# Second pair's K^T K apart from K^T Q, larger first loads, a shorter norm root, a clamp on another engine, and a redrawn order

## The chip, the core and the metric

The kernel runs on one core of a Trainium2 chip. The core has a matrix engine (TensorE, PE in the profile, with PEld for its weight loads), VectorE (DVE), ScalarE (ACT), GpSimd (POOL) and SyncE (SP), which here only issues DMA transfers. POOL issues DMA transfers too. Each engine works through its own instructions in order and waits on semaphores for the others. The metric is the time of one execution on the device in microseconds (us).

## The reference

A layer of linear attention with the delta rule, and behind it a gated causal convolution:

```python
B, H, S, D = 4, 8, 768, 48
k_n = k / (norm(k, axis=-1) + 1e-6)
for t in range(S):
    y[:, :, t] = einsum('bhd,bhde->bhe', q[:, :, t], state)
    v_old = einsum('bhde,bhd->bhe', state, k_n[:, :, t])
    state += beta[t] * outer(k_n[t], v[t] - v_old)
x = y.transpose(0, 2, 1, 3).reshape(4, 768, 384)
gate = sigmoid(sum_k conv_w[k] * shift(x, 4 - k))        # 5 taps, causal, per channel
out = (gate * (x @ w_val)) @ w_out
```

The convolution's and the output layers' weights arrive as float64, as pairs of 32-bit words, and are put together as fp32 on the chip.

## The kernel before, in words

**Tiling.** The 768 tokens are cut into 12 chunks of 64, two chunks are a pair (six pairs, `NG`). The 32 sequences (4 batches of 8 heads) fill the partitions and the free axis. Within a chunk the recurrence is solved as a triangular system; between chunks the state is carried.

**The stages of a pair `g`** (names as in the code):

- `grams`: K^T K and K^T Q of both chunks on PE. For pairs under `NAL` (only pair 0) they are separate products (`kp`, `qp`); for the others one joint product (`kq`, two per chunk, each with K as the stationary side and K and Q side by side as the moving side). ACT copies K^T K into `GL` (`kpevac`, `kqevac`), DVE multiplies K^T Q by a mask into `AQ` (`att0`, `att`). For pair 0 DVE realigns parts of `GL` (`kpfix`); for the others SP does it by DMA (`realign`).
- `prep`, nearly all on DVE: a transposition of `GL` into `TLP` (`trans_in`), then 18 small steps on 128x32 (`coef`), which take the norm's inverse root by three Newton steps of three operations each and make the coefficients, then `cscale`, `row`, `mergez8`, `merget8`, which invert the small triangular blocks, and two transpositions (`trans_out`) into `XA` and `WB`. ACT (pair 0) or POOL (other pairs) copies them on as `XAB` (`xblocks`) and `W` (`wblocks`); SP writes the diagonal blocks of `GL` into `G` (`gblocks`).
- `tri`, per chunk: the products `m16`, `m32`, `lev1`, `lev2` on PE with ACT copies between them; they end in `XX`.
- `chain`, per chunk: `e` (K times state, PE), `eadd` (DVE), `u` (PE, `XX` times V), `s` (the next state, PE), `y` (PE), ACT copies between them, and six small DMA transfers by SP (kind `Lx`) that put patches of `YSB` into x (`X`).
- `moe`, per pair: five taps of the convolution (one as an ACT copy, four as DVE operations on three blocks each), sigmoid on ACT, `val` on PE, `gate` on DVE, `outp` on PE, `oevac` on ACT, output by SP.

**The weights** (`plan_weights`, seven of them: the convolution's, 128x15, then three blocks each of `w_val` and `w_out`, 128x384): SP loads the words, then `f64_bits` runs step 0 on ACT and steps 1 to 4 on DVE (step 1 is a clamp by max and min), `f64_low` runs on ACT, and `f64_join` on POOL. Two buffers are used in turn, taken from `X`, `OS` and `GT`.

**Loads.** K and Q of a chunk come in halves of 48x512 (96 KB each, `load_k`, `load_q`), four DMA transfers each. The first four chunks (`NSP`) are loaded by SP, the later ones by POOL.

**What sets the order.** All operations are collected in a plan and numbered. The list `ORDER` gives the order in which they are emitted, for all engines at once, and `BANKS` gives the bank of PSUM of each product. An entry of -1 in `ORDER` emits one small matmul on constants (`keep_warm`); the list before has none. In the trace each fp32 matmul counts as two.

Of the kernel before, what the change touches and what calls it, by code (L numbers as in the profile page):

```python
# [19 lines left out]
NP = 16  # L20
NU = 32
HB = 8
NAL = 1
# [88 lines left out]
]  # L112
BANKS = (
    "2301451005500150542334121020310011111441044230325245334254224345034420352123140133255103053104224032150552400423"
    "013100412454031514230541552034323314055305340203512432524224043210012143115341040405012052022053124"
)


# [931 lines left out]
```

## Time and profile before

| | |
|---|---|
| runs | 312.48, 313.34, 319.33 us; median 313.34 |
| profiled execution | 315.52 us, its span 313.8 us |
| granted PE clock, mean | 0.88 |
| busy: PE, PEld | 258.8 us (82%), 194.6 us (62%) |
| busy: DVE, ACT, POOL | 215.5 us (69%), 168.5 us (54%), 115.2 us (37%) |
| HBM read, written | 21.35 MB, 4.72 MB |

The shares are means over the span; the stages differ. The timeline views list an instruction's start and length, and in square brackets the time that its engine had been idle before it and what ended that idle time. The windows view gives the busy time of each engine in a stretch, beside the PE clock that was granted in it (1.00 is the full clock, 0.50 the half).

### The profile page before, as it was taken

To read this page: it belongs to the slowest core of one execution; us is meant where nothing else is said; L and a number is where in the kernel's file an instruction comes from. 1 tells how busy PE (TensorE), PEld (TensorE's weight loads), DVE (VectorE), ACT (ScalarE), POOL (GpSimd) and SP (SyncE) were. 2 spreads that over 40 slices of the span, in tenths; PEclk is the share of its full clock that TensorE was granted. 3 is DMA by queue.
4 is the path that set the end of the run, shared out by engine and by line. 5 is a ranking of instruction groups with operands and counts; after the bars stand their busy time and mean duration, and the time that the engine had idled before them with its cause. 6 is when DMAs were issued, how large, how long until landed. Compare 5 with 4: busy or idle time off the path is not lost.

```text
span 313.8 us, 14806 instructions
## 1 busy us (share of the span) xinstructions
PE 258.8 (82%) x6422; PEld 194.6 (62%) x6422; DVE 215.5 (69%) x504; ACT 168.5 (54%) x404; POOL 115.2 (37%) x230
## 2 busy tenths in 40 slices
PE   7410996567679897999997899898999799999994
PEld 4310885457555576965767875577657598656772
DVE  5799539996479897289983099993999701664480
ACT  1900666556559544484555477354666446774531
POOL 8844207244516393502669102767012451000000
PEclk9855577567999999599999799999999857999999
DMA  5697727363558464534586535873226272304033
GB/s 152 177 221 184 207 48 194 100 157 67 134 138 167 96 173 115 148 73 115 134 227 150 133 59 122 251 168 75 56 81 157 79 173 55 92 17 119 15 101 75
DMA packets 55937, 39.29 MB, mean 125 GB/s; under 512 B 38592, under 2 KB 46912, under 8 KB 55872
## 3 DMA queue, kind: packets, MB, share of 16 engines
q1 hardware_dynamic: 50752, 25.76, 33.8%
q0 software_dynamic: 5120, 12.59, 15.4%
q8 instruction: 50, 0.82, 1.2%
q14 instruction: 15, 0.12, 0.1%
HBM read 21.35 MB, written 4.72 MB: 83 GB/s over the span
## 4 chain that ended last, share of the span: by engine, by line
PE 48%; DVE 4%; ACT 3%; DMA 3%; issue 2%; SPq 2%; POOL 2%; ACTq 0%; POOLq 0%; DVEq 0%
PE PB L242 23%; PE PB L688 13%; PE PB L697 10%; SPq L229 2%; DMA X<-YSB 2%; DMA Y<-US 2%; PE SPS L242 1%; ACT Y L224 1%; DVE PR L490 1%; POOL XAB L226 1%; ACT OS L224 1%; DVE PR L502 1%; DVE VT L623 1%; ACT X L224 0%; DVE TT__81 L483 0%
## 5 line engine op out<-in xcount | busy, mean ns | idle before, releaser
L679 DVE SCALAR_TENSOR_TENSOR GT<-X,CW,GT 128x512 f32<-128x512 f32 (+1 forms) x84 | 54.0, 678 | 15.5 <-ACT GT L224 14.4
L242 PE MATMUL PB<-KQ 48*64 48x128 f32 (+1 forms) x896 | 35.7, 310 | 18.9 <-DMA KQ<-in_kf_dram 14.2
L697 PE MATMUL PB<-WO,GT 128*128 128x384 f32 x144 | 50.7, 497 | 0.7 <-DVE GT L692 0.7
L688 PE MATMUL PB<-X,WV 128*128 128x512 f32 (+1 forms) x126 | 49.7, 541 | 1.7 <-DMA X<-YSB 1.7
L224 ACT ACTIVATE XX<-PB 32x512 f32<-32x512 f32 (+1 forms) x72 | 36.9, 518 | 22.3 <-PE PB L242 21.5
L242 PEld LDWEIGHTS PB<-KQ 48*64 48x64 f32 x896 | 30.4, 168 | 21.9 <-issue 15.5
L405 DVE TENSOR_TENSOR AQ<-PB,MASK 128x256 f32<-128x256 f32 (+1 forms) x44 | 18.5, 442 | 31.7 <-ACT GL L224 15.7
L697 PEld LDWEIGHTS PB<-WO,GT 128*128 128x128 f32 x144 | 26.1, 189 | 16.8 <-DVE GT L692 1.3
L688 PEld LDWEIGHTS PB<-X,WV 128*128 128x128 f32 x126 | 22.9, 190 | 19.9 <-issue 15.5
L571 POOL TENSOR_TENSOR VT<-VT,NRM 128x384 f32<-128x384 f32 x24 | 20.6, 859 | 26.9 <-DMA VT<-in_vt_dram 14.0
L224 ACT ACTIVATE Y<-SPS 64x384 f32<-64x384 f32 (+1 forms) x44 | 20.4, 482 | 16.9 <-PE SPS L242 16.6
L242 PE MATMUL PB<-KQ,Y 112*48 112x64 f32 (+2 forms) x768 | 28.1, 236 | 0.1
L242 PEld LDWEIGHTS PB<-KQ,Y 112*48 112x48 f32 (+2 forms) x768 | 25.7, 136 | 2.5 <-issue 1.3
L623 DVE TENSOR_TENSOR VT<-PB,VT 128x384 f32<-128x384 f32 x22 | 11.5, 547 | 22.2 <-PE PB L242 22.2
L242 PE MATMUL PB<-YS,W 128*64 128x64 f32 x384 | 18.0, 258 | 5.5 <-issue 2.1
L232 POOL DMA_DIRECT2D VT<-in_vt_dram x16 | 9.0, 566 | 34.0 <-PE PB L242 22.7
L242 PEld LDWEIGHTS PB<-YS,W 128*64 128x64 f32 x384 | 16.1, 169 | 7.6 <-issue 3.4
L242 PE MATMUL PB<-XAB,G 128*64 128x32 f32 x384 | 16.8, 249 | 4.2 <-POOL XAB L226 3.7
L224 ACT ACTIVATE X<-PB 112x256 f32<-112x256 f32 (+1 forms) x24 | 11.6, 488 | 16.1 <-PE PB L242 13.7
L232 POOL DMA_DIRECT2D KQ<-in_kf_dram x32 | 16.8, 527 | 8.8 <-PE PB L242 8.6
L224 ACT ACTIVATE GL<-PB 128x256 f32<-128x256 f32 (+1 forms) x44 | 16.1, 396 | 6.6 <-PE PB L242 5.2
L242 PEld LDWEIGHTS PB<-XAB,G 128*64 128x64 f32 x384 | 15.9, 171 | 5.5 <-POOL XAB L226 4.6
(106 smaller groups left out, 462.6 us busy)
## 6 DMA issues: line engine op xcount, KB each, us to landing
KQ<-AQ SPq DMA_DIRECT2D x48, 128.0 KB, 3.2
out_dram<-OS SPq DMA_DIRECT2D x20, 192.0 KB, 2.1
KQ<-in_kf_dram POOLq DMA_DIRECT2D x32, 96.0 KB, 4.2
KQ<-in_qr_dram POOLq DMA_DIRECT2D x32, 96.0 KB, 3.7
VT<-in_vt_dram POOLq DMA_DIRECT2D x16, 192.0 KB, 4.3
KT<-in_kt_dram POOLq DMA_DIRECT2D x16, 192.0 KB, 4.1
Y<-US SPq DMA_DIRECT2D x24, 96.0 KB, 2.8
KQ<-in_kf_dram SPq DMA_DIRECT2D x16, 96.0 KB, 2.6
```

The source lines that it names most:

```text
L224: A.activation(out=out, in_=in_, func=AF.Copy, **kw)
L226: eng.tensor_copy(out=out, in_=in_)
L229: SP.dma_start(out=dst, in_=src)
L232: G.dma_start(out=dst, in_=src)
L242: PE.matmul(p, lhsT, rhs, start=start, stop=stop, tile_position=(row, col), skip_group_check=True)
L405: V.tensor_tensor(out=AQ[ch % NAQ][:, HB * h + u:HB * h + u + n], in0=p, in1=MASK[h].unsqueeze(1).to_broadcast([128, n, C]), op=ALU.mult)
L490: V.tensor_tensor(out=pr[:, b], op=ALU.mult, in0=l16[:, b, 8:16, 4 * kb:8].unsqueeze(1).to_broadcast([128, 4, 8, n]), in1=t16[:, b, 4 * kb ...
L571: G.tensor_tensor(out=v, in0=v, in1=n.unsqueeze(2).to_broadcast([128, HB, D]), op=ALU.mult)
L623: V.tensor_tensor(out=v, in0=bank["e", ch, h][:, 0:HB * D], in1=v, op=ALU.add)
L679: V.scalar_tensor_tensor(out=g, in0=XB[p % NX][:, m, :, lo + k:lo + k + n], scalar=CW[:, m, k:k + 1], in1=g, op0=ALU.mult, op1=ALU.add)
L688: PE.matmul(d[:, 0:B * n], WV[:, k, 128 * m:128 * m + 128], XB[p % NX][:, k, :, lo + 4:lo + 4 + n], start=k == 0, stop=k == NKT - 1)
L697: PE.matmul(bank["out", p, lo, i][:, 0:DM], g[:, i] if n == 2 * C else g[:, 2 * i:2 * i + 2].rearrange("p b t -> p (b t)"), WO[:, k, :], s ...
```

## The change

1. `NAL` is 2: pair 1 has separate K^T K and K^T Q products as well (`kp`, `qp`), 64 matmuls more than before (128 of 64x64 in place of 64 of 64x128). Its realignment stays with SP's DMA transfers, but they now wait for the two chunks' K^T K only.
2. The first four chunks' K and Q are loaded whole (192 KB, 48x1024): 16 SP transfers fewer.
3. The norm root takes one step of third order and one Newton step in place of three Newton steps: 16 operations on DVE in place of 18 for each pair. The coefficients are scaled so that the factors stand in the later steps.
4. Step 1 of `f64_bits`, the clamp, runs on POOL instead of DVE, for all seven weights.
5. `ORDER` and `BANKS` are drawn anew. The list has 1530 entries in place of 1562, and four of them are `keep_warm`, which stand before the `u` of chunk 5, behind the `s` of chunk 5, behind the `m32` of chunk 6 and before the `lev2` of chunk 8.

```diff
--- before.py
+++ after.py
@@ -20,7 +20,7 @@
 NP = 16
 NU = 32
 HB = 8
-NAL = 1
+NAL = 2
 NSP = 4
 QB = 4
 DM = H * D
@@ -36,83 +36,81 @@
 STORE = [LATE + EARLY, EARLY + LATE]
 
 ORDER = [
-    227, 25, 29, 0, 23, 24, 21, 22, 26, 11, 16, 40, 41, 37, 38, 39, 36, 35, 34, 356, 43, 42, 164, 47, 45, 44, 264, 49,
...
 ]
 BANKS = (
...
 )
 
 
@@ -297,7 +295,7 @@
         if step == 0:
             A.activation(out=a, in_=hi.bitcast(F32), func=AF.Abs, scale=2.0 ** 16)
         if step == 1:
-            V.tensor_scalar(out=a, in0=a, scalar1=F64_LO, scalar2=F64_HI, op0=ALU.max, op1=ALU.min)
+            G.tensor_scalar(out=a, in0=a, scalar1=F64_LO, scalar2=F64_HI, op0=ALU.max, op1=ALU.min)
         if step == 2:
             V.tensor_scalar(out=ai, in0=ai, scalar1=3, scalar2=None, op0=ALU.logical_shift_left)
         if step == 3:
@@ -323,7 +321,7 @@
         hold = SCRATCH[slot]
         add("SP", load, (SCR[slot][:, 0:2 * n].bitcast(U32), src.bitcast(U32)), r=first if i else [], w=[raw, *hold], kind="Lw")
         for step in range(5):
-            add("DVE" if step else "ACT", f64_bits, (n, slot, step), r=[raw, *hold], w=[parts], 
+            add(("ACT", "POOL", "DVE", "DVE", "DVE")[step], f64_bits, (n, slot, step), r=[raw, *hold], w=[parts], 
                 kind=f"f64_{step}" + "c" * (not i))
         add("ACT", f64_low, (w, n, slot), r=[raw, *hold], w=[to], kind="f64_low" + "c" * (not i))
         for step in range(2):
@@ -427,24 +425,30 @@
                             op0=ALU.logical_shift_right, op1=ALU.bitwise_xor)
         if step == 2:
             V.tensor_scalar(out=ROOT, in0=ROOT, scalar1=ROOT_SEED, scalar2=None, op0=ALU.mult)
-        if step in (3, 6, 9):
+        if step in (3, 7):
             V.tensor_tensor(out=QUOT, in0=ROOT, in1=ROOT, op=ALU.mult)
-        if step in (4, 7, 10):
-            V.scalar_tensor_tensor(out=QUOT, in0=QUOT, scalar=-0.5, in1=SQ, op0=ALU.mult, op1=ALU.mult)
-        if step in (5, 8, 11):
+        if step == 4:
+            V.tensor_tensor(out=QUOT, in0=QUOT, in1=SQ, op=ALU.mult)
+        if step == 5:
+            V.scalar_tensor_tensor(out=QUOT, in0=QUOT, scalar=-10.0 / 3.0, in1=QUOT, op0=ALU.add, op1=ALU.mult)
+        if step == 6:
+            V.scalar_tensor_tensor(out=ROOT, in0=QUOT, scalar=5.0, in1=ROOT, op0=ALU.add, op1=ALU.mult)
+        if step == 8:
+            V.scalar_tensor_tensor(out=QUOT, in0=QUOT, scalar=-0.5 * 0.375 * 0.375, in1=SQ, op0=ALU.mult, op1=ALU.mult)
+        if step == 9:
             V.scalar_tensor_tensor(out=ROOT, in0=QUOT, scalar=1.5, in1=ROOT, op0=ALU.add, op1=ALU.mult)
+        if step == 10:
+            V.scalar_tensor_tensor(out=ROOT, in0=SQ, scalar=0.375, in1=ROOT, op0=ALU.mult, op1=ALU.mult)
+        if step == 11:
+            V.tensor_scalar(out=ROOT, in0=ROOT, scalar1=1e-6, scalar2=None, op0=ALU.add)
         if step == 12:
-            V.tensor_tensor(out=ROOT, in0=SQ, in1=ROOT, op=ALU.mult)
+            V.tensor_tensor(out=QUOT, in0=ROOT, in1=ROOT, op=ALU.mult)
         if step == 13:
-            V.tensor_scalar(out=ROOT, in0=ROOT, scalar1=1e-6, scalar2=None, op0=ALU.add)
+            V.reciprocal(out=QUOT, in_=QUOT)
         if step == 14:
-            V.tensor_tensor(out=QUOT, in0=ROOT, in1=ROOT, op=ALU.mult)
-        if step == 15:
-            V.reciprocal(out=QUOT, in_=QUOT)
-        if step == 16:
             V.scalar_tensor_tensor(out=ct, in0=BE[:, g * NU:(g + 1) * NU], scalar=-1.0, in1=QUOT,
                                    op0=ALU.mult, op1=ALU.mult)
-        if step == 17:
+        if step == 15:
             V.transpose(out=nrm, in_=ROOT)
 
     def trans_in(g):
@@ -732,16 +736,19 @@
 
     first = [("first", q) for q in range(0, 128, 32)]
 
+    def parts(ch):
+        return [(range(2), slice(0, NP))] if ch < NSP else [([h], slice(HB * h, HB * h + HB)) for h in range(2)]
+
     def load_k(ch):
-        for h in range(2):
+        for hs, u in parts(ch):
             for f in (0, 64):
-                fetch(KF[ch % NKF][f:f + D, HB * h:HB * h + HB], kf[ch, f // 64, :, HB * h:HB * h + HB], ch, [("KF", ch % NKF, h, f)], "LKF")
+                fetch(KF[ch % NKF][f:f + D, u], kf[ch, f // 64, :, u], ch, [("KF", ch % NKF, h, f) for h in hs], "LKF")
 
     def load_q(ch):
-        for h in range(2):
+        for hs, u in parts(ch):
             for v in range(2):
                 to = 64 - 64 * v
-                fetch(R[ch % NR][to:to + D, v, HB * h:HB * h + HB], qr[ch, 1 - v, :, HB * h:HB * h + HB], ch, [("R", ch % NR, "Q", v, h)], "LQR",
+                fetch(R[ch % NR][to:to + D, v, u], qr[ch, 1 - v, :, u], ch, [("R", ch % NR, "Q", v, h) for h in hs], "LQR",
                       r=[("Rz", ch % NR)] + (first if ch < 2 else []))
 
     def k_of(ch):
@@ -771,7 +778,7 @@
                 for h in range(2):
                     w = [("GL", gb, h, ch % 2, i) for i in range(2)]
                     add("ACT", kpevac, (ch, h), r=[toks[h]], w=w, give=[toks[h]])
-                    for a in range(2):
+                    for a in range(0 if g else 2):
                         add("DVE", kpfix, (ch, h, a), r=[toks[h], *w], w=[("GD", gb, h, a, ch)], give=[toks[h]])
             for ch in (2 * g, 2 * g + 1):
                 toks = [("qp", ch, h) for h in range(2)]
@@ -792,19 +799,19 @@
         gb = g % 2
         gl = lambda h: [("GL", gb, h, c, i) for c in range(2) for i in range(2)]
         def plan_coef():
-            for step in range(18):
-                r = ["CF"] + (["TL"] if step == 0 else []) + (["BE"] if step == 16 else [])
+            for step in range(16):
+                r = ["CF"] + (["TL"] if step == 0 else []) + (["BE"] if step == 14 else [])
                 w = ["CF"]
-                if step == 17:
+                if step == 15:
                     w.append(("NRM", gb))
-                if step == 16:
+                if step == 14:
                     w.append(("CT", gb))
                 add("DVE", coef, (g, step), r=r, w=w)
 
-        for h in range(0 if g < NAL else 2):
+        for h in range(2 if g else 0):
             for a in range(2):
                 add("SP", realign, (g, h, a), r=gl(h), w=[("GD", gb, h, a)])
-        add("DVE", trans_in, (g,), r=gl(0) + gl(1) + [("GD", gb, h, a, *([c] if g < NAL else [])) for h in range(2) for a in range(2) for c in range(2)], w=["TL"])
+        add("DVE", trans_in, (g,), r=gl(0) + gl(1) + [("GD", gb, h, a, *([] if g else [c])) for h in range(2) for a in range(2) for c in range(2)], w=["TL"])
         for q in range(0, 128, 32):
             add("SP", gblocks, (g, q), r=gl(0) + gl(1) + ["G64z"], w=[("G64", q)] + ([] if g else [("first", q)]))
         plan_coef()
```

How the order changes is shown at three places. The first is DVE behind the first pair's `trans_out` (`WB<-TT__81`). `TLP<-GL_71` is `trans_in` of the second pair, the AQ rows are masked products, and the rows on `OS` and `X_90` are steps 1 to 4 of the weights. Before:

```order
L511 STREAM_TRANSPOSE XA<-TT__81 128x16x32
L511 STREAM_TRANSPOSE WB<-TT__81 128x16x32
L405 TENSOR_TENSOR AQ_66<-PB_117,MASK_108 128x256
L405 TENSOR_TENSOR AQ_66<-PB_118,MASK_108 128x256
...
L300 TENSOR_SCALAR X_90<-X_90 128x384
L302 TENSOR_SCALAR X_90<-X_90 128x384
L304 SCALAR_TENSOR_TENSOR X_90<-X_90 128x384
L307 TENSOR_SCALAR X_90<-X_90 128x384
L452 STREAM_TRANSPOSE TLP<-GL_71 128x1024
L424 TENSOR_SCALAR SQ<-TLP 128x32
```

and with the change (L298 is now the clamp on POOL, L300, L302 and L305 the three steps left on DVE):

```order
L515 STREAM_TRANSPOSE XA<-TT__81 128x16x32
L515 STREAM_TRANSPOSE WB<-TT__81 128x16x32
L456 STREAM_TRANSPOSE TLP<-GL_71 128x1024
L403 TENSOR_TENSOR AQ_67<-PB_114,MASK_107 128x512
L300 TENSOR_SCALAR OS<-OS 128x384
L300 TENSOR_SCALAR X_90<-X_90 128x384
L403 TENSOR_TENSOR AQ_66<-PB_118,MASK_107 128x512
L302 SCALAR_TENSOR_TENSOR X_90<-X_90 128x384
L305 TENSOR_SCALAR X_90<-X_90 128x384
L403 TENSOR_TENSOR AQ_67<-PB_116,MASK_108 128x512
L422 TENSOR_SCALAR SQ<-TLP 128x32
```

The second pair's transposition has moved from behind sixteen rows to directly behind `WB`.

The second place is POOL's queue with the change, at the last K load of chunk 4 (`KQ<-in_kf_dram` in the last row but one; L298 is the clamp, L312 a join of the weights, `KQ<-in_qr_dram` a Q load):

```order
L575 TENSOR_TENSOR VT_64<-VT_64,NRM_99 128x384
L230 DMA KQ<-in_qr_dram 48x512
L237 MEMSET XX_74 32x8x32 x2
L298 TENSOR_SCALAR OS<-OS 128x384
L298 TENSOR_SCALAR X_90<-X_90 128x384
L312 TENSOR_TENSOR WV<-WV,X_90 128x384
L230 DMA KQ<-in_qr_dram 48x512
L312 TENSOR_TENSOR WV<-WV,X_90 128x384
L230 DMA KQ<-in_kf_dram 48x512
L237 MEMSET XX_76 32x8x32
```

Before, the eight loads of chunk 4 stood together in front of all weights:

```order
L232 DMA KQ<-in_kf_dram 48x512 x2
L232 DMA KQ<-in_qr_dram 48x512
L232 DMA KQ<-in_kf_dram 48x512
L232 DMA KQ<-in_qr_dram 48x512
L239 MEMSET XX_75 32x8x32
L232 DMA KQ<-in_kf_dram 48x512
L232 DMA KQ<-in_qr_dram 48x512
L239 MEMSET XX_75 32x8x32
L232 DMA KQ<-in_qr_dram 48x512
L571 TENSOR_TENSOR VT_65<-VT_65,NRM_99 128x384
```

So the last K load of chunk 4 has moved behind two clamps and two joins.

The third place is PE behind the `s` of chunk 9, where the last pair's `m16` of chunks 10 and 11 come (`XAB,G_72`). `KQ,Y_69` is a y product of chunk 9, `YS,W_73` an `m32`, `XX_75,GL_71` a `lev1`, `Y_68,KQ` the e product of chunk 10. Before:

```order
L242 MATMUL SPS_113<-US_79,KT_63 48x48
L242 MATMUL PB_116<-XAB,G_72 64x32 x16
L242 MATMUL PB_114<-XAB,G_72 64x32 x16
L242 MATMUL PB_115<-KQ,Y_69 48x64 x16
L242 MATMUL PB_118<-YS,W_73 64x64 x16
L242 MATMUL PB_117<-XX_75,GL_71 32x32 x32
L242 MATMUL PB_116<-KQ,Y_69 48x64 x16
L242 MATMUL PB_118<-YS,W_73 64x64 x16
L242 MATMUL PB_115<-Y_68,KQ 64x48
```

and with the change (`WO,GT` is an output product; the e product's rows alternate between two banks and are cut):

```order
L240 MATMUL SPS_113<-US_79,KT_63 48x48
L240 MATMUL PB_114<-KQ,Y_69 48x64 x16
L240 MATMUL PB_115<-KQ,Y_69 48x64 x16
L701 MATMUL PB_117<-WO,GT 128x384 x3
L240 MATMUL PB_119<-Y_68,KQ 64x48
L240 MATMUL PB_118<-Y_68,KQ 64x48
...
L240 MATMUL PB_114<-XAB,G_72 64x32 x16
L240 MATMUL PB_115<-XAB,G_72 64x32 x16
L240 MATMUL PB_119<-YS,W_73 64x64 x16
L701 MATMUL PB_114<-WO,GT 128x384 x3
L240 MATMUL PB_119<-XX_75,GL_71 32x32 x32
```

Both y products of chunk 9, an output product and the e product of chunk 10 have moved ahead of the two `m16`.

## Rows read from the trace of the kernel before

**Rows 1.** The page: span, and part 1 (busy time, share, instructions).

```profile
span 313.8 us, 14806 instructions
...
PE 258.8 (82%) x6422; PEld 194.6 (62%) x6422; DVE 215.5 (69%) x504; ACT 168.5 (54%) x404; POOL 115.2 (37%) x230
```

**Rows 2.** Windows: stretch, length, busy us (instructions) by engine, granted clock, DMA, GB/s.

```profile
core 0: us, PE busy (x) PEld busy (x) DVE busy (x) ACT busy (x) POOL busy (x), PEclk, DMA share, GB/s
14.00:31.00 17.00, 2.06 (x61) 1.82 (x59) 15.91 (x54) 1.62 (x4) 8.55 (x22) 0.50 0.89 213
35.30:75.50 40.20, 29.10 (x896) 26.87 (x896) 30.25 (x76) 25.33 (x65) 13.23 (x18) 0.64 0.52 132
75.50:92.30 16.80, 12.17 (x449) 10.76 (x449) 7.69 (x14) 8.63 (x22) 6.74 (x14) 1.00 0.47 111
92.30:122.30 30.00, 27.98 (x662) 18.23 (x664) 27.24 (x66) 18.92 (x43) 15.79 (x23) 1.00 0.63 154
249.50:262.10 12.60, 11.63 (x271) 11.12 (x265) 0.04 (x1) 5.89 (x15) 6.46 (x12) 0.50 0.66 166
```

**Rows 3.** Timeline of PE: start, us, instruction, count, idle before and its releaser.

```profile
30.99 3.81 PE L242 MATMUL PB<-KQ 48*64 48x128 f32 x64 [14.18 <-DMA KQ<-in_kf_dram]
...
35.28 1.92 PE L242 MATMUL PB<-XAB,G 128*64 128x32 f32 x32 [0.48 <-issue]
...
37.13 3.69 PE L242 MATMUL PB<-KQ 48*64 48x128 f32 x64
...
46.12 1.10 PE L242 MATMUL PB<-KQ 48*64 48x128 f32 x32
...
52.03 1.96 PE L242 MATMUL PB<-VT,XX 64*64 64x48 f32 x64
...
58.43 1.98 PE L242 MATMUL PB<-KQ 48*64 48x128 f32 x32
...
253.92 1.93 PE L242 MATMUL PB<-KQ,Y 128*48 128x64 f32 x32
```

**Rows 4.** Timeline of DVE, the same columns.

```profile
17.48 0.32 DVE L300 TENSOR_SCALAR X<-X 128x15 f32<-128x15 f32 x1
...
33.67 1.02 DVE L511 STREAM_TRANSPOSE WB<-TT__81 128x512 f32<-128x512 f32 x1
...
45.60 0.36 DVE L300 TENSOR_SCALAR OS<-OS 128x384 f32<-128x384 f32 x1 [2.73 <-ACT OS L298]
...
47.59 1.14 DVE L300 TENSOR_SCALAR X<-X 128x384 f32<-128x384 f32 x1
...
51.21 1.97 DVE L452 STREAM_TRANSPOSE TLP<-GL 128x1024 f32<-128x1024 f32 x1
...
55.05 0.19 DVE L435 SCALAR_TENSOR_TENSOR ROOT<-QUOT,ROOT 128x32 f32<-128x32 f32 x1
...
55.28 0.19 DVE L431 TENSOR_TENSOR QUOT<-ROOT 128x32 f32<-128x32 f32 x1
...
73.16 1.05 DVE L511 STREAM_TRANSPOSE XA<-TT__81 128x512 f32<-128x512 f32 x1
...
86.70 0.75 DVE L679 SCALAR_TENSOR_TENSOR GT<-X,CW,GT 128x512 f32<-128x512 f32 x1 [3.16 <-ACT GT L224]
```

**Rows 5.** POOL: one join's timeline row; two groups by line and form.

```profile
47.52 1.00 POOL L314 TENSOR_TENSOR WV<-WV,GT 128x384 f32<-128x384 f32 x1 [10.70 <-ACT ZS L224]
...
L226 POOL COPY W<-WB 32x256 f32<-32x256 f32 x24 | 9.4, 392 | 12.5 <-DVE WB L511 11.2 <-DVE NRM L448 0.3
...
L314 POOL TENSOR_TENSOR WO<-WO,X 128x384 f32<-128x384 f32 x4 | 4.4, 1111 | 4.3 <-DVE X L307 4.3
```

**Rows 6.** The page, part 6: DMA issues, KB each, us to landing.

```profile
KQ<-in_kf_dram POOLq DMA_DIRECT2D x32, 96.0 KB, 4.2
```

**Rows 7.** Timeline of SP's DMA issues.

```profile
79.39 2.51 SPq L229 DMA_DIRECT2D X<-YSB  x4
...
82.57 3.87 SPq L229 DMA_DIRECT2D X<-YSB  x5
```

**Rows 8.** Timeline of ACT, the first stretch.

```profile
6.56 1.28 ACT L224 ACT_TABLE_LOAD   x1 [6.56 <-DVE G L239]
```

**Rows 9.** ACT by line and form: busy, mean ns, idle before.

```profile
L224 ACT ACTIVATE GT<-X,CW 128x512 f32<-128x512 f32 x15 | 10.6, 721 | 4.7 <-DMA X<-YSB 4.5 <-ACT ZS L224 0.2
```

More of the change, by code (lines that the diff above doesn't have):

```diff
@@ L38 @@
 ORDER = [
[73 rows of a table removed]
[71 rows of a table added]
 ]
 BANKS = (
-    "2301451005500150542334121020310011111441044230325245334254224345034420352123140133255103053104224032150552400423"
-    "013100412454031514230541552034323314055305340203512432524224043210012143115341040405012052022053124"
+    "2301304511013430210545022521033330132150052501423542153420502144335404502055025340134125153411401310044250325105"
+    "435451535245013444005215355432102345044302430212320551211250132112311004554215453233054451304050321"
 )
```

143 rows, old and new, of the table ORDER are left out of this document.

## The prediction

> **What bounds the kernel now.** I read the page's totals first. TensorE (PE) is busy for 82% of the span, VectorE (DVE) for 69% [rows 1], but these are averages over stages with different limits, so I cut the span into stretches [rows 2]. The reader should see three kinds. From 14.0 to 31.0 us DVE works nearly all the time and PE for 2.1 of 17.0 us: the coefficient and triangular steps of the first pair, with PE waiting. From 35.3 to 92.3 us no engine is full: PE has 29.1 of 40.2 us at a granted clock of 0.64, then 12.2 of 16.8: a chain that hops between engines. From 92.3 us on PE is nearly full (28.0 of 30.0 in the stretch shown) and DVE close behind it (27.2); the exception is 249.5 to 262.1 us, where PE is busy 11.6 of 12.6 us but at the half clock. So time can be had in the first 92 us and at that last boundary; elsewhere both engines would have to shed work together.
>
> Then I followed the chain in the PE and DVE timelines. DVE ends the first pair's last output transposition (WB) at 33.67 + 1.02 = 34.69 us [rows 4]; call that moment T. PE starts `m16` of chunk 0 at 35.28 us, but runs the joint products `kq` of chunk 2 just before it (30.99 us, 3.81 us long, after waiting 14.18 us for a K load) and those of chunk 3 right behind it (37.13, 3.69 us), all in front of the first `u`, which ends at 53.99 us [rows 3], T + 19.3. The second pair's XA transposition ends at 74.21 us, T + 39.5; the first tap of the convolution starts at 86.70, 12.5 us later, having waited 3.16 us [rows 4].
>
> I make the sum against the profiled execution, 315.5 us (span 313.8 [rows 1]). That stands 2.2 us above the median of 313.3 and within the three runs (312.5 to 319.3); I correct nothing for it. About 2%, 6.3 us, is what a measurement of this kernel can tell from no change.
>
> **A, the first pair: 1.3 us.** The norm root has two steps fewer. Such a step occupies DVE from 55.05 to the next one's start at 55.28 us [rows 4], so 2 x 0.23 = 0.46. The clamp of the convolution's weights (0.32 at 17.48 us [rows 4]) leaves DVE while DVE is what everything waits for. The whole loads spare issues, and ACT's table load, which waits for VectorE's memset of G until 6.56 us [rows 8], comes earlier; I estimate 0.5 for this. Bounds: 0.5 (the steps alone) to 1.8.
>
> **B, from T to the second pair's output: 3.5 us.** With K^T K apart from K^T Q, the products of chunks 2 and 3 run ahead of T. The 64 additional matmuls (two for each joint one) cost nothing: PE is idle 15 of 17 us there [rows 2]. If that cover were gone they would cost up to 7.5, what the two joint groups take now. What leaves the stretch behind `m16`: 3.69 us at 37.13 us and, as chunk 4 now comes later, 1.10 at 46.12 us [rows 3]. The interval of 18.7 us from 35.28 to 53.99 us thus becomes 13.9, and `u` of chunk 0 ends near T + 14.5.
>
> I don't credit the 4.8 us in full, for the next thing is late: chunk 4's last K load now stands in POOL's queue behind two weight clamps and joins. A join of this size took 1.00 at 47.52 us and a W copy 0.39 on average [rows 5]; four of the former and a few of the latter behind T make the issue T + 12 or so, and such a load lands 4.2 us later [rows 6], at T + 16. From `kq` of chunk 4 to the second XA's end it took 74.21 - 58.43 = 15.8 us [rows 3, 4]; add 2.0 for the other half of chunk 4's `kq` (1.98 per half [rows 3]) and 2.8 for chunk 1's level products, which stood ahead before. That is T + 36 against T + 39.5. On DVE the second pair's big transposition (1.97 at 51.21 us) now follows WB directly instead of standing 17 us later; it needs SP's realigning transfers, which are covered as long as they land by T. What queues behind it: the masked products, the weights' steps and the coefficient steps, and if the transfers are late all of these wait. Bounds for B: 0 (chunk 4's load eats all) to 6 (DVE's early transposition counts in full).
>
> A clamp on POOL of 128x384 shows in no row. The nearest is the join's 1.00; a copy of 256 columns at 0.39 gives 0.6 for 384 as the lower end [rows 5]. I take 1.0, because it is the same shape on the same engine in this stretch. VectorE does the same in 0.36 alone and in 1.14 when POOL's join runs beside it (45.60 and 47.59 us [rows 4], 47.52 us [rows 5]). The Trainium skill, page "GPSIMD Engine Reference", section "Engine selection", sends an elementwise operation on a tile to VectorE, and calls GpSimd about 2x slower for two inputs and roughly line-rate for one; by that the clamp (one input) would last about as long as on VectorE, and B would win another 1.3 us for the two of them. The trace agrees on the two-input half only (0.36 against 1.00); no run here shows the other yet.
>
> **C, the x patches of pair 1: 2.2 us.** The first tap waits 3.16 us for ACT's convolution copy [rows 4], and those copies wait 4.5 us in all for the patches that SP writes [rows 9]: these are issued in groups at 79.39 (2.51 us) and 82.57 (3.87 us), with other issues between [rows 7]. In the new order chunk 0's six stand ahead of chunk 1's second y product and unmixed; of the 3.16 us I take 2.2. Bounds 0 to 4.
>
> **D, two coefficient steps fewer in pairs 2 to 5: 1.0 us.** 4 x 0.46 = 1.8 is spared where DVE has 27.2 of 30.0 us in one such stretch [rows 2]; PE is as full, so I take about half. Bounds 0 to 1.8.
>
> **E, the last boundary: 3.0 us.** From 249.5 to 262.1 us PE ran at the half clock: 11.63 us that are 5.8 at the full one, so no more than 12.6 - 5.8 = 6.8 can come back [rows 2]. Now both y products of chunk 9 (1.93 for one at 253.92 us, half clock [rows 3]), an output product and the e product of chunk 10 stand between chunk 9's s and chunk 10's `m16`. Work that is done anyway fills a wait: at the full clock 1.0 for each of the three, the e product taken as long as a y product, is 3.0 us. Bounds 0 to 6.8.
>
> **At nothing:** 16 SP issues fewer (SP waits there), the four warming matmuls, the bigger loads (the DMA engines are busy 0.89 of the first stretch at 213 GB/s either way [rows 2]), and the first pair's gram blocks, now behind the realigning transfer in SP's queue: they have some 10 us before `m16`. If SP were late there, the wait would show on `m16` directly.
>
> Sum: 315.5 - 1.3 - 3.5 - 2.2 - 1.0 - 3.0 = **304.5 us**. The spread of the bounds, taken half to either side as they are independent, gives 298 to 308.5.
>
> **Rivals.**
>
> 1. *The early gain ends at the first full stage.* From 92.3 us on PE and DVE are both full; if C, D and E give nothing, only A + B = 4.8 stay: 310.7 us, no change. For it: 28.0 of 30.0 us PE [rows 2]. Against it: a stage that begins earlier ends earlier.
>
> 2. *The weights' chain becomes the path; the slower one.* Weight load, ACT, POOL clamp, DVE, POOL join, POOL's load of chunk 4, `kq`, ACT, then `s`: all in POOL's and DVE's order. Where the clamp takes longer than the 1.0 assumed, each us costs 2 in the first pair (two clamps ahead of the load) and up to 4 over two pairs. The 11 us are gone with a clamp of nearly 4 us; with 5 us, 16 to 17 are lost and the time is about 320. For it: the DVE step that tripled to 1.14 beside POOL [rows 4]. Against: POOL's joins of this shape have means of 1.00 to 1.11 [rows 5].
>
> 3. *PE's clock stays down longer.* Between the first and second XAB product PE now has less to do (7.5 us less, in a stretch that shows 29.1 of 40.2 us at 0.64 [rows 2]). If the half clock lasts into 75.5 to 92.3 us, whose 12.17 us are now at 1.00, the 12.17 become up to 24.3 and fill the stretch and 7.5 us more: 304.5 + 7.5 = 312, no change. For it: the clock fell after PE's idle 14 to 31 us, where the row reads 0.50. Against: chains in 92 to 250 us hold 1.00 with PE nearly full. The Trainium skill, page "TensorE: Matmul & The Clock Gate", section "HAM oscillation", describes bursts between waits that start cold again and again; this stretch's 0.64 agrees.
>
> **Numbers.** Forecast 0.58, rival 1 0.22, rival 2 0.10, rival 3 0.10. The range reaches from the forecast's low end, 298, over rivals 1 and 3 to 313; outside are rival 2 and the tails. Faster by over 2% means under 307: of the forecast 0.54, of rival 1 0.06, together 0.60. Within 2%: 0.04 + 0.16 + 0.10 = 0.30. Slower: 0.10.
>
> **What the profile after would show.** A: WB ends near 33.4 us. B: the second big transposition starts directly behind WB; PE has no joint products between `m16` of chunk 0 and its first `u`, which ends near 48; PE's wait ahead of chunk 4's products is ended by a POOL load; the second XA ends near 69.5. C: the first tap starts near 79.5, its wait under 1 us. E: the stretch from chunk 9's s product to chunk 10's last level product is about 3 us shorter. Rival 2 shows as POOL clamps over 2 us, rival 3 as a granted clock under 0.8 between the second XA and the first tap, rival 1 as the lead of 5 to 7 us at the first tap that has shrunk at the start of the third pair. The prediction is wrong if WB ends later than 35 us, or if the lead at the first tap isn't there at 250 us.

## The result, and the profile after

The changed kernel takes 305.18 us (median of 4 runs, 303.75 to 305.45), before 314.83 in the same comparison; the ratio is 0.9708 with a 95% interval of 0.9622 to 0.9795. The forecast was 304.5, faster, within 298 to 313. The time came out as said, but most of it came from another place than the prediction named.

The page of the changed kernel, its span and busy times and the granted clock in 40 slices (tenths of full speed), answers to [rows 1]:

```profile
span 303.7 us, 15029 instructions
...
PE 259.6 (85%) x6558; PEld 195.0 (64%) x6558; DVE 209.4 (69%) x481; ACT 168.4 (55%) x400; POOL 126.0 (42%) x237
...
PEclk9855575767697999999999999999599999999999
```

PE is about as busy as before in a span that is 10.1 us shorter, so over the whole span what went is waiting. To see where, I cut both spans at the same two products, the end of chunk 3's `s` and of chunk 9's. The windows of before (the columns of [rows 2]):

```profile
0.00:117.90 117.90, 78.74 (x2221) 62.91 (x2221) 89.51 (x222) 60.96 (x142) 56.99 (x122) 0.78 0.60 148
117.90:250.00 132.10, 122.22 (x3198) 89.40 (x3198) 100.11 (x235) 75.38 (x185) 51.92 (x97) 0.96 0.51 125
250.00:313.80 63.80, 57.79 (x1004) 42.25 (x1004) 25.88 (x49) 32.20 (x77) 6.24 (x12) 0.90 0.33 85
```

and of the change:

```profile
0.00:119.40 119.40, 86.29 (x2360) 69.94 (x2361) 86.97 (x213) 62.06 (x140) 66.29 (x129) 0.76 0.64 147
119.40:242.40 123.00, 117.51 (x3198) 86.25 (x3197) 94.21 (x219) 74.00 (x183) 49.58 (x91) 0.97 0.53 132
242.40:303.70 61.30, 55.79 (x1010) 38.77 (x1010) 28.27 (x52) 32.33 (x77) 10.17 (x19) 0.99 0.33 89
```

The first stretch got 1.5 us longer, the middle 9.1 shorter, the last 2.5 shorter: together the 10.1. PE's idle time (length less busy) in the middle fell from 9.9 to 5.5 us; the other 4.7 us of the 9.1 are PE being busy for less time with as many matmuls (122.22 and 117.51 us for 3198 records each). The idle time goes with the order in the profiled executions of the kernels below too: 4.1 to 5.8 us in seven with the change's list, 9.9 and 10.8 in two with before's, this one and clamp_pool_alone; early_only and middle_only, which mix the lists, lie between (7.6 and 7.3). The clock doesn't: clamp_pool_alone ran the order of before at 1.00 and took 127.4 us for the middle instead of 132.1.

```profile
119.30:246.70 127.40, 116.60 (x3202) 84.27 (x3198) 99.67 (x234) 75.14 (x185) 50.73 (x96) 1.00 0.51 128
```

One boundary between pairs shows how; before from 163.5 to 182 us, then the change from 161 to 179 us, each around the `m16` of chunk 6:

```profile
163.50:182.00 18.50, 15.45 (x531) 14.09 (x528) 4.73 (x11) 10.76 (x27) 9.07 (x17) 0.91 0.57 140
```

```profile
161.00:179.00 18.00, 17.32 (x546) 14.12 (x540) 9.15 (x18) 10.90 (x29) 11.54 (x22) 1.00 0.55 134
```

VectorE worked 9.15 us there instead of 4.73, and PE 17.32 at the full clock instead of 15.45 at 0.91. Here the redrawn order has put a y product, which waits for nobody, and an `m32` ahead of chunk 6's `e`. Two of the four warming matmuls stand in this stretch too; no_warm below, which has none, keeps PE busy for 17.24 of 17.9 us there. The Trainium skill, page "TensorE: Matmul & The Clock Gate", section "HAM oscillation", describes bursts of matmuls that start cold again after each wait. The trace agrees in this pair (0.91 with 3.05 us idle, 1.00 with 0.68), but not everywhere: clamp_pool_alone, in before's order, went through this boundary at 1.00 with 2.84 us idle.

```profile
163.30:181.80 18.50, 15.66 (x587) 13.95 (x579) 7.31 (x15) 12.07 (x31) 9.12 (x17) 1.00 0.56 142
```

Single executions differ. Up to chunk 3's `s`, before's order took 116.7 to 122.0 us in four executions, and the change's 116.7 to 119.4 in three, so the 1.5 us by which the first stretch got longer are no finding. Ratios and their intervals go by the fast runs of each kernel, medians and ranges by all of them, and the profiled executions of late_only, last_boundary and load_halves were slow ones, so of these I use single rows only where they repeat what other kernels show. Kernels that were timed in different comparisons are set against each other by their ratios to before, and the closest pairs are those of one comparison: late_only, early_only, no_warm and clamp_dve are one such group, last_boundary, gram_copies_first, two_steps_more and clamp_dve_copies_first another.

### The profile page after: what moved, and what is told of

Its sections match the earlier page's. It is cut to its first block, busy times and chain, and to the rows that moved or that the text cites. A ratio compares the mean times of both kernels' runs of the same rounds, so it can differ in the third digit from the quotient of the medians.

```text
span 303.7 us, 15029 instructions
## 1 busy us (share of the span) xinstructions
PE 259.6 (85%) x6558; PEld 195.0 (64%) x6558; DVE 209.4 (69%) x481; ACT 168.4 (55%) x400; POOL 126.0 (42%) x237
## 4 chain that ended last, share of the span: by engine, by line
PE 61%; DMA 11%; ACT 6%; POOL 6%; DVE 6%; issue 5%; SPq 4%; ACTq 0%; POOLq 0%; DVEq 0%
PE PB L240 27%; PE PB L692 15%; PE PB L701 15%; SPq L227 4%; DMA W<-WB 4%; PE SPS L240 3%; ACT XX L222 2%; DMA X<-in_conv_w_dram 2%; DMA X<-in_w_val_dram 2%; DMA KQ<-in_qr_dram 2%; DMA X<-in_w_out_dram 1%; POOL KQ L230 1%; ACT Y L222 1%; POOL KQ L237 1%; DVE AQ L403 1%
## 5 line engine op out<-in xcount | busy, mean ns | idle before, releaser
L683 DVE SCALAR_TENSOR_TENSOR GT<-X,CW,GT 128x512 f32<-128x512 f32 (+1 forms) x84 | 57.7, 710 | 16.0 <-DMA Y<-US 7.4
L692 PE MATMUL PB<-X,WV 128*128 128x512 f32 (+1 forms) x126 | 50.9, 548 | 0.0
L240 PE MATMUL PB<-KQ 48*64 48x64 f32 (+1 forms) x1024 | 36.6, 297 | 13.1 <-DMA KQ<-in_qr_dram 7.2
L240 PEld LDWEIGHTS PB<-KQ 48*64 48x64 f32 x1024 | 31.6, 174 | 16.8 <-POOL IND L261 4.1
L701 PEld LDWEIGHTS PB<-WO,GT 128*128 128x128 f32 x144 | 26.2, 189 | 16.4 <-DVE GT L696 0.6
L403 DVE TENSOR_TENSOR AQ<-PB,MASK 128x256 f32<-128x256 f32 (+1 forms) x40 | 18.1, 469 | 15.6 <-PE PB L240 10.7
L222 ACT ACTIVATE Y<-SPS 64x384 f32<-64x384 f32 (+1 forms) x44 | 20.7, 482 | 13.0 <-PE SPS L240 12.6
L240 PE MATMUL PB<-XAB,G 128*64 128x32 f32 x384 | 15.2, 239 | 7.7 <-ACT XAB L222 6.0
L240 PE MATMUL PB<-VT,XX 64*64 64x48 f32 x768 | 16.3, 235 | 5.7 <-DVE VT L627 3.3
L222 ACT ACTIVATE Y<-PB 64x192 f32<-64x192 f32 x48 | 14.5, 321 | 11.1 <-PE PB L240 10.7
L240 PEld LDWEIGHTS PB<-VT,XX 64*64 64x64 f32 x768 | 14.4, 149 | 9.6 <-issue 6.9
L230 POOL DMA_DIRECT2D KT<-in_kt_dram x16 | 8.9, 557 | 27.2 <-PE SPS L240 26.8
L240 PEld LDWEIGHTS PB<-XAB,G 128*64 128x64 f32 x384 | 14.3, 158 | 8.5 <-issue 6.3
```

The lines of the kernel that those rows point to most:

```text
L222: A.activation(out=out, in_=in_, func=AF.Copy, **kw)
L230: G.dma_start(out=dst, in_=src)
L240: PE.matmul(p, lhsT, rhs, start=start, stop=stop, tile_position=(row, col), skip_group_check=True)
L403: V.tensor_tensor(out=AQ[ch % NAQ][:, HB * h + u:HB * h + u + n], in0=p, in1=MASK[h].unsqueeze(1).to_broadcast([128, n, C]), op=ALU.mult)
L683: V.scalar_tensor_tensor(out=g, in0=XB[p % NX][:, m, :, lo + k:lo + k + n], scalar=CW[:, m, k:k + 1], in1=g, op0=ALU.mult, op1=ALU.add)
L692: PE.matmul(d[:, 0:B * n], WV[:, k, 128 * m:128 * m + 128], XB[p % NX][:, k, :, lo + 4:lo + 4 + n], start=k == 0, stop=k == NKT - 1)
```

## Experiments

"Order of before" and "of the change" stand for the two lists; operations are carried over by name, and PSUM banks are those of the list an operation comes from, or a free one where that is taken.

### Which part of the order

**late_only**

```diff
 ORDER = [
     # before's, up to s of chunk 3
-    # then before's
+    # then the change's (operations of before throughout)
```

> The operations of before, in the order of before until the s product of chunk 3 (about 118 us), and from there on in the order of the change. Theory O (the redrawn order of the later pairs made the gain: of the 10.1 us of span, idle PE and half clock behind 120 us count 13.0, and the stretch before lost 2.9): 301 to 305 us. Rival P (the edits of the first stages made it, and their lead is only seen later): 312 to 317, as before.

305.6 us (303.18 to 308.17), ratio 0.9654 (0.9561 to 0.9747). With no edit of the first stages and with three Newton steps the later order alone (its warming matmuls included) gives 10.9 us, as much as the whole change in its own comparison (0.9708), and two thirds of what no_warm, the change without four small matmuls, gives in this one (0.9505). Theory O holds for the larger part of the gain.

**early_only**

```diff
 ORDER = [
     # the change's, up to s of chunk 3
-    # then the change's
+    # then before's (operations of the change throughout)
```

> The operations of the change, in its order until the s product of chunk 3, and from there on in the order of before, without the four warming matmuls. Theory O: no gain is left, 314 to 319 us. Rival P: most of the gain stays, 303 to 308.

310.2 us (309.45 to 310.32 and one outlier of 415.86), ratio 0.9815 (0.973 to 0.9901): neither number. There is a gain of some 6 us (3 to 8.5 by the interval) that theory O doesn't give. Its stretches:

```profile
0.00:119.20 119.20, 87.05 (x2349) 70.59 (x2349) 88.18 (x212) 61.11 (x138) 67.60 (x129) 0.73 0.65 149
119.20:245.80 126.60, 118.96 (x3199) 86.29 (x3198) 95.24 (x221) 75.19 (x185) 50.73 (x96) 0.99 0.51 126
245.80:308.30 62.50, 54.40 (x1008) 38.16 (x1004) 25.88 (x49) 32.20 (x77) 6.83 (x13) 0.99 0.33 89
```

It isn't a lead at chunk 3's `s` (119.2 against 117.9 us). The middle is 5.5 us shorter in the same order, at a clock of 0.99, but clamp_pool_alone, all in before's order and no faster than before, also has a middle of 127.4 us, at 1.00. So this profile doesn't show where the 6 us come from: the cause stays open. With late_only's 10.9 us they make 16.7, and no_warm gains 15.6 in the same comparison, so the two parts about add up.

**middle_only**

```diff
 ORDER = [
     # before's, up to s of chunk 3
-    # then before's
+    # then the change's, up to u of chunk 9
     # then before's
```

> The operations of before in its order until the s product of chunk 3, then the order of the change until the u product of chunk 9, then the order of before again. Theory M (the redrawn order between the two makes most of the gain, by less idle PE and less half clock there): 9 to 11 us below before, near 305 to 307, and 123 to 124 us from chunk 3's s to chunk 9's s instead of 132. Rival (the gain of the later order sits behind chunk 9, in the last boundary): 312 to 316.

310.33 us (307.71 to 316.07), ratio 0.9874 (0.9835 to 0.9913): 4 us, less than half of what was expected. **last_boundary** is its counterpart:

```diff
 ORDER = [
     # before's, up to u of chunk 9
-    # then before's
+    # then the change's
```

> The operations and the order of before until the u product of chunk 9, and from there on the order of the change: term E by itself. As forecast (real products fill the wait ahead of chunk 10): 3.0 us less than before, bounds 0 and 6.8, and no half clock between chunk 9's s and chunk 10's levels. Rival (the half clock there comes and goes with the run, and the order doesn't matter): the same as before within 1%.

314.51 us, ratio 0.9959 (0.9912 to 1.0007): term E by itself is 1.3 us, with an interval from nothing to 2.8. The last stretches of the two, middle_only and then last_boundary:

```profile
243.40:307.30 63.90, 55.97 (x1004) 40.31 (x1004) 25.80 (x49) 32.01 (x77) 5.80 (x11) 0.93 0.28 75
```

```profile
256.40:318.00 61.60, 55.63 (x1014) 38.80 (x1010) 28.30 (x51) 32.30 (x77) 10.16 (x19) 1.00 0.33 89
```

Behind chunk 9 the order goes with the length: 62.5 (early_only) to 64.8 us (clamp_pool_alone) with before's, 60.6 to 61.6 with the change's. But 4.0 and 1.3 don't add up to late_only's 10.9 (1 - 0.9654 of 315). The two parts may belong together: the order of the change leaves output products for the last boundary, and these are missing further ahead unless that part is filled otherwise too. That link is read from the lists and not shown, and late_only was timed in another comparison; which single moves in the middle pay was not tried.

### The warming matmuls

```diff
             if n < 0:
-                keep_warm()
+                pass
```

> The change without its four warming matmuls. Theory O (the clock stays up since real products fill the boundaries): 304 to 306 us, the same stretches of half clock. Rival W (the warming matmuls keep the clock up): at least one more stretch of half clock behind 120 us, 307 to 312.

303.46 us (299.32 to 319.73), ratio 0.9505 (0.9416 to 0.9594). The middle of the profiled run, the shortest of the four, is at the full clock throughout:

```profile
116.70:236.30 119.60, 113.82 (x3190) 83.07 (x3189) 93.83 (x219) 73.76 (x183) 49.05 (x91) 1.00 0.54 136
```

The clock stays up without them, and no cost of leaving them out shows: they count as nothing, as forecast, and rival W falls. The longest run, 319.73 us, had a mean clock of 0.78; it has no profile.

### The clamp

**clamp_dve**

```diff
-            G.tensor_scalar(out=a, in0=a, scalar1=F64_LO, ...)
+            V.tensor_scalar(out=a, in0=a, scalar1=F64_LO, ...)
-            add(("ACT", "POOL", "DVE", "DVE", "DVE")[step], f64_bits, ...)
+            add(("ACT", "DVE", "DVE", "DVE", "DVE")[step], f64_bits, ...)
```

> The change with the clamp of the weights on VectorE again, nothing else. The clamp took 1.49 us on POOL, and two of them stand ahead of the Q loads of chunk 5, for which PE waits 1.37 and 1.85 us. Theory C (the clamp on POOL costs what these waits show): 300 to 303.5 us and the two waits gone. Rival D (VectorE is what these stretches wait for, and seven operations of 0.36 to 1.14 us come onto it): 305 to 309.

298.08 us (296.27 to 300.71), ratio 0.9448 (0.9357 to 0.9539), against 0.9708 for the change. By these ratios the clamp on POOL costs some 8 us, but they come from two comparisons. Pairs within one comparison give less: no_warm, with the clamp on POOL, has 0.9505, 1.8 us more than clamp_dve, and gram_copies_first and clamp_dve_copies_first below, which differ by the clamp alone, have medians of 304.37 and 297.43 us and profiled spans of 297.0 and 293.3. So it costs between 2 and 8 us. The time lies below theory C's range, but the cost of 2 to 5 us that theory C named isn't excluded; rival D falls. POOL's timeline of the change shows the queue:

```profile
75.46 1.49 POOL L298 TENSOR_SCALAR OS<-OS 128x384 f32<-128x384 f32 x1
77.02 0.39 POOL L224 COPY W<-WB 32x256 f32<-32x256 f32 x1
77.51 0.58 POOL L230 DMA_DIRECT2D KQ<-in_kf_dram  x1
78.14 0.39 POOL L224 COPY W<-WB 32x256 f32<-32x256 f32 x1
78.49 1.00 POOL L230 DMA_DIRECT2D KQ<-in_kf_dram  x2
79.56 1.49 POOL L298 TENSOR_SCALAR X<-X 128x384 f32<-128x384 f32 x1
81.03 0.82 POOL L575 TENSOR_TENSOR VT<-VT,NRM 128x384 f32<-128x384 f32 x1
81.81 0.59 POOL L230 DMA_DIRECT2D KQ<-in_qr_dram  x1
```

PE of the change waits for these Q loads, in two rows:

```profile
87.76 0.50 PE L240 MATMUL PB<-KQ 48*64 48x128 f32 x4 [1.37 <-DMA KQ<-in_qr_dram]
90.11 3.05 PE L240 MATMUL PB<-KQ 48*64 48x128 f32 x60 [1.85 <-DMA KQ<-in_qr_dram]
```

and clamp_dve's PE timeline has the same products without that wait:

```profile
86.89 0.44 PE L240 MATMUL PB<-KQ 48*64 48x128 f32 x5
87.83 2.06 PE L240 MATMUL PB<-KQ 48*64 48x128 f32 x59 [0.51 <-issue]
```

In the five other profiled kernels with this queue the two waits make 1.1 to 2.1 us together, in the three with the clamp on VectorE they are gone. Another wait repeats more closely: VectorE waits 9.29 us for POOL's scaling of V, the row at 81.03 above (8.79 to 9.88 at this operation in those five), and in clamp_dve 3.01 (2.54 and 3.49 in the other two):

```profile
78.48 0.56 DVE L627 TENSOR_TENSOR VT<-PB,VT 128x384 f32<-128x384 f32 x1 [3.01 <-POOL VT L575]
...
85.43 3.65 DVE L683 SCALAR_TENSOR_TENSOR GT<-X,CW,GT 128x512 f32<-128x512 f32 x5 [3.26 <-ACT GT L222]
```

The stretches of clamp_dve, cut at the same products, are 115.2, 121.0 and 61.1 us; so 4.2 of the 6.4 us of span come back ahead of chunk 3's `s`, and most of the rest in the middle:

```profile
0.00:115.20 115.20, 83.29 (x2357) 67.45 (x2358) 87.50 (x219) 61.97 (x140) 56.71 (x122) 0.78 0.67 153
115.20:236.20 121.00, 116.88 (x3200) 86.25 (x3199) 92.09 (x219) 73.77 (x183) 49.28 (x91) 0.97 0.54 134
```

The first stretches of gram_copies_first and clamp_dve_copies_first, with the clamp on POOL and on VectorE, differ as much, by 4.0 us, and the two stretches behind by 0.4 and 0.1 us:

```profile
0.00:115.80 115.80, 86.75 (x2357) 69.86 (x2359) 86.50 (x212) 61.86 (x140) 65.90 (x128) 0.73 0.66 151
```

```profile
0.00:111.80 111.80, 82.29 (x2357) 66.52 (x2358) 88.08 (x219) 62.12 (x140) 57.36 (x123) 0.79 0.67 158
```

**clamp_pool_alone** asks whether the clamp costs by itself:

```diff
-            V.tensor_scalar(out=a, in0=a, scalar1=F64_LO, ...)
+            G.tensor_scalar(out=a, in0=a, scalar1=F64_LO, ...)
-            add("DVE" if step else "ACT", f64_bits, ...)
+            add(("ACT", "POOL", "DVE", "DVE", "DVE")[step], f64_bits, ...)
```

> Before with one part of the change alone: the clamp of the weights on POOL, everything else and the order as before. Theory C (the clamp's 1.49 us in POOL's queue and in the weights' chain cost time wherever they stand ahead of loads and scalings): 2 to 7 us above before, 316 to 321. Rival (it costs only in the new order, which puts two clamps ahead of chunk 5's Q loads): within 1% of before.

314.28 us, ratio 1.0018 (0.9963 to 1.0073): nothing that shows in before's order, though each clamp is as long. So the length alone isn't the cost; with the waits above, the loads and scalings that the new order puts behind the clamps are. By line and form, of this kernel:

```profile
L300 POOL TENSOR_SCALAR X<-X 128x384 f32<-128x384 f32 x3 | 4.5, 1494 | 2.5 <-ACT X L298 2.5
```

### The first pair and the smaller parts

**gram_copies_first**

```diff
 ORDER = [  # ACT: kpevac 43 and 53 ahead of f64_low 160 of the convolution's weights
-    ... 160 ... 43 ... 53 ...
+    ... 43, 53, 160 ...
```

> The change with ACT's last two copies of the first pair's K^T K moved ahead of the step of the convolution's weights, for whose load ACT waited 2.17 us. Theory A (that wait is why the first pair wasn't earlier): its last output transposition ends near 32.5 us instead of 35.28. If the lead lasts, 302 to 303.5 us; rival (the next waits, the second pair's realigning transfers and POOL's loads, eat it): 304.5 to 306.

304.37 us (298.70 to 305.53). ACT's timeline of the change shows the cause, a wait for the convolution weights' load ahead of the last two copies:

```profile
8.79 0.60 ACT L222 ACTIVATE GL<-PB 128x512 f32<-128x512 f32 x1
11.55 0.21 ACT L308 ACTIVATE CW<-X 128x15 f32<-128x15 uint32 x1 [2.17 <-DMA X<-in_conv_w_dram]
...
12.85 1.06 ACT L222 ACTIVATE GL<-PB 128x512 f32<-128x512 f32 x2
```

With the copies first, VectorE's timeline reads

```profile
13.49 1.98 DVE L456 STREAM_TRANSPOSE TLP<-GL 128x1024 f32<-128x1024 f32 x1
...
33.16 1.01 DVE L515 STREAM_TRANSPOSE WB<-TT__81 128x512 f32<-128x512 f32 x1
```

so the first transposition starts 1.8 us earlier than the change's 15.29, but T, the end of WB, comes at 34.17, 1.1 us earlier and not the 2.8 expected. In the time the lead can't be told from nothing.

**two_steps_more**

```diff
+        if step in (9, 10):
+            V.tensor_scalar(out=ROOT, in0=ROOT, scalar1=1.0, scalar2=None, op0=ALU.mult)
```

> The change with two more steps of 128x32 on VectorE in each pair's coefficients (multiplications by one), as many as the norm root had before. As forecast (A's share 0.46 and D 1.0): 1.5 us more, 306 to 307.5. Rival (VectorE is not what ends the later stages): 304.5 to 305.7; the first pair's output 0.4 to 0.5 later under both.

304.39 us (300.40 to 308.39), ratio 0.9541 (0.9467 to 0.9615): not above the change. The rival holds as far as it can be told: the shorter norm root is worth nothing that shows, but four runs that spread over 8 us can't exclude the 1.5 us of the forecast.

**load_halves**

```diff
+    def load_halves(dst, src):
+        n = dst.shape[1]
+        for u in range(0, n, HB):
+            SP.dma_start(out=dst[:, u:u + HB], in_=src[:, u:u + HB])
-        add(*(("SP", load) if ch < NSP else ...
+        add(*(("SP", load_halves) if ch < NSP else ...
```

> The change with the first four chunks' K and Q loaded in halves of 96 KB again, 16 DMA transfers more on SP. As forecast (the bigger loads count as nothing): 304 to 306 us and the first pair's last output transposition within 0.5 us of 35.3. Rival (halves land earlier, or their issues of 0.43 us delay the queue by up to 6.9 us): the transposition ends 1 us or more earlier or later.

305.97 us (297.93 to 311.20); T at 36.75 in its one profiled run, 1.5 us later. The time is the change's; whether T is really later is left open by one run.

**clamp_dve_copies_first** joins both edits (the two diffs above).

> Both edits on the change: the clamp on VectorE, and ACT's two copies first. If the two are independent: 298.1 less 2 to 3, so 295 to 296.5 us. If the first pair's lead is eaten by the next wait (the realigning transfers, for which VectorE waited 3.33 us with the clamp on VectorE): 297 to 299.

297.43 us (295.13 to 302.43), ratio 0.9393 (0.9329 to 0.9458). It is faster than before and than the change; against clamp_dve the second edit brings 0.7 us by the medians and 1.7 by the ratios, which can't be told from nothing.

**realign_first** adds to it

```diff
 ORDER = [  # SP: gram blocks 65, 66, 64 of pair 0, then the realigning transfers of pair 1, in one row
-    ... 252 ... 65 ... 66 ... 64 ... 251 ... 225 ... 249 ... 223 ... 163 ... 250 ...
+    ... 65, 66, 64, 252, 251, 249, 250 ... 225 ... 223 ... 163 ...
```

> The change with the clamp on VectorE, ACT's two copies first, and SP's realigning transfers of the second pair issued one after the other behind the first pair's gram blocks, ahead of the attention stacks. Theory B (the second pair's transposition, which waited 2.66 us for the last of them, then starts right behind WB, and the lead lasts): the transposition starts near 34.5 us instead of 37.2, and 293 to 296 us. Rival (the wait isn't on the path, the same time): 296.5 to 299.

296.53 us (295.70 to 300.36), ratio 0.9488 (0.9432 to 0.9544). The second big transposition starts right behind WB:

```profile
34.09 1.00 DVE L515 STREAM_TRANSPOSE WB<-TT__81 128x512 f32<-128x512 f32 x1
34.94 1.87 DVE L456 STREAM_TRANSPOSE TLP<-GL 128x1024 f32<-128x1024 f32 x1
```

instead of 37.18, and the time stays within 1 us of the version without it (by the ratios, from two comparisons, it is 3 us behind). The wait was real, and taking it away gains nothing that shows.

## Why the prediction came out right, and where it was wrong

**A (1.3 us) failed.** T is 35.28, not 33.4. VectorE's own part held: from the first transposition to T it takes 19.99 us instead of 20.72, 0.73 less where 0.78 was forecast for the steps and the clamp. But it starts 1.32 us later, before and then with the change:

```profile
13.97 1.96 DVE L452 STREAM_TRANSPOSE TLP<-GL 128x1024 f32<-128x1024 f32 x1
```

```profile
15.29 1.95 DVE L456 STREAM_TRANSPOSE TLP<-GL 128x1024 f32<-128x1024 f32 x1
```

The further rows of VectorE of the change:

```profile
34.28 1.00 DVE L515 STREAM_TRANSPOSE WB<-TT__81 128x512 f32<-128x512 f32 x1
37.84 1.98 DVE L456 STREAM_TRANSPOSE TLP<-GL 128x1024 f32<-128x1024 f32 x1 [2.55 <-DMA GL<-GL]
...
70.67 1.05 DVE L515 STREAM_TRANSPOSE XA<-TT__81 128x512 f32<-128x512 f32 x1
...
81.89 0.56 DVE L627 TENSOR_TENSOR VT<-PB,VT 128x384 f32<-128x384 f32 x1 [9.29 <-POOL VT L575]
...
85.95 3.64 DVE L683 SCALAR_TENSOR_TENSOR GT<-X,CW,GT 128x512 f32<-128x512 f32 x5
```

I looked at what VectorE spares and not at ACT's queue, where the convolution weights' step had moved ahead of two copies that VectorE needs. With these first (gram_copies_first) 1.1 of the missing 1.9 us come back.

**B (3.5 us) held as an interval.** The second XA ends at 71.72 us, T + 36.4, where T + 36 was said (before T + 39.5 [rows 3, 4]). Its inner steps were off: the first `u` ends at 51.71 us, T + 16.4, where T + 14.5 was said, and what follows took less than I gave it.

```profile
49.75 1.96 PE L240 MATMUL PB<-VT,XX 64*64 64x48 f32 x64 [1.32 <-ACT XX L222]
```

The transposition waited 2.55 us for SP, and the clamp took 1.49 us instead of the 1.0 I chose from the joins [rows 5]; the true value lay above both rows that I had bounded it by.

**C (2.2 us) failed.** The first tap no longer waits, but starts at 85.95 us, 0.75 earlier than before [rows 4] and not 7. VectorE has by then waited 9.29 us for POOL's scaling of V, which stands behind the two clamps. Nor did the new order of the patches end the tap's own wait: in clamp_dve, where the wait for V is 3.01 us, the tap waits 3.26 us for ACT's convolution copy, as before, and starts at 85.43. So the lead of 7 us that I gave A, B and C together had shrunk to 0.75 at the first tap and doesn't show at chunk 3's `s` (1.5 us behind, within what executions differ by).

**Rival 2 was half there.** I gave it a chance of 0.10 and priced each us over 1.0 at up to 4; the extra 0.49 us then makes 2. The clamp on POOL as a whole cost between 2 and 8. Its mechanism is right and the point from which it decides was wrong: not the clamp's length but what the order puts behind it (clamp_pool_alone costs nothing that shows). The Trainium skill's "GPSIMD Engine Reference", section "Engine selection", calls one-input operations roughly line-rate on GpSimd; the trace disagrees (1.49 against VectorE's 0.36 [rows 4]). Its advice, VectorE for an elementwise operation, is what paid. The prediction had set 0.36 against 1.00 as the two-input case; 0.36 is VectorE's clamp, with one input, so the two aren't the same operation.

**The step that failed most** is in the first paragraph: "elsewhere both engines would have to shed work together", and with it D, 1.0 us for the whole middle. The middle gave 9.1 us in the profile, and none of it that shows by two coefficient steps (two_steps_more). I read 28.0 of 30.0 us busy in one stretch [rows 2] as a full engine and took that for all pairs; the boundaries between the pairs, where before has 15.45 of 18.5 us at 0.91, I didn't cut out, apart from the last. I showed only one redrawn boundary in the order and priced only that one, though the list was redrawn throughout.

**E (3.0 us)** was about right in size: the last stretch is 2.5 us shorter in the profile, at a clock of 0.99 instead of 0.90, and 1.3 (0 to 2.8) when it is done alone. Its sum was not: it fills a wait with 3.0 us of products, where PE is idle for only 1.0 of the 12.6 us [rows 2], and of the 2.5 us that came 2.0 are PE's busy time (57.79 and 55.79) and 0.5 idle time. **Rival 1** fell, since the lead of clamp_dve at chunk 3's `s` (4.2 us against the change) is 6.4 at the end. **Rival 3** showed its sign, a granted clock under 0.8 between the second XA and the first tap; before, then with the change:

```profile
74.20:86.70 12.50, 8.74 (x362) 8.03 (x358) 4.42 (x11) 7.58 (x18) 7.91 (x15) 0.99 0.44 100
```

```profile
71.70:85.95 14.25, 11.80 (x368) 11.26 (x371) 4.85 (x9) 8.63 (x21) 13.34 (x21) 0.76 0.41 93
```

PE needs 3.1 us more there for about as many matmuls. How much of the missing lead that is, beside the wait for V, no run separates. The parts costed at nothing held, within what the runs resolve.

So the sum was right by two errors: 7.0 us forecast ahead of chunk 3's `s` that don't show there, and 9.1 in the middle where 1.0 was forecast. That they cancelled was luck. By one of the signs that the prediction set itself, WB ending later than 35 us, it was wrong (35.28), and the spread that it gives around the forecast doesn't follow from its bounds: half of each, added up, gives 299.8 to 309.8 and not 298 to 308.5.

## What to carry to other kernels

Where a hand-ordered schedule is redrawn, cut the trace at every repeat of the boundary and price each one; a mean of 93% busy hides several waits of one to two us, and a clock that is sometimes slower around them. An operation that moves to an engine which also issues loads is priced by what stands behind it in that queue, not by its length. And look at the queue of the engine that feeds the bottleneck: a lead on the bottleneck engine that its feeder doesn't share is not a lead.

## What was unexpected about the hardware

A clamp of 128x384 on POOL (max and min with constants, one input) took 1.49 us, longer than a join of two inputs of that shape (1.00 to 1.11 [rows 5]) and four times VectorE's 0.36. And TensorE's clock did not follow from the order: between chunk 3's and chunk 9's `s` the order of before ran at 0.96 with 9.9 us idle in one execution and at 1.00 with 10.8 us idle in another (clamp_pool_alone), 132.1 and 127.4 us long.
